# A new instruction order for a fused linear-attention and SoLU kernel: first loads and ScalarE's first logarithm moved

## Chip, cores and metric

The kernel runs on one core of a Trainium2 chip. The metric is the device time of one execution in microseconds (us), the median of several runs.

## The reference

Two layers. The first is a recurrent attention in the manner of RWKV-6 on B=4, H=8, S=768, D=48; the second a feed-forward layer with a SoLU activation and a layer norm on the 3072 tokens of 384 features that the first one gives.

```python
for t in range(S):
    kt, vt, rt, wt = (k[:, :, t], v[:, :, t], r[:, :, t], w[:, :, t])
    cur = np.einsum('bhd,bhe->bhde', u[None] * kt, vt)
    y[:, :, t] = np.einsum('bhd,bhde->bhe', rt, state + cur)
    state = wt[:, :, :, None] * state + np.einsum('bhd,bhe->bhde', kt, vt)
...
h = x @ w_in                                  # 384 -> 1024
e = np.exp(h - h_max)
sm = e / (np.sum(e, axis=-1, keepdims=True) + 1e-09)
solu = h * sm
ln = (solu - mu) / np.sqrt(var + 1e-06) * g_ln
return (ln @ w_out).astype(np.float32)        # 1024 -> 384
```

## The kernel before

The sequence is cut into six chunks of 128 tokens; a chunk of one batch is a unit, so there are 24 units (0 to 23). Units 0 to 3 are the first chunk of the four batches and have no state from before. Within a unit the recurrence is written as matrix products: prefix sums of the logarithm of w give decays, which scale k and r; masked products of r and k give a 128x128 score matrix for each head; a state of one 48x48 matrix for each head goes from chunk to chunk.

Every step of a unit is a small function (a stage), and a text that lists them one by one, `ORDER`, says in which order all stages are put into the program. A word of it is a stage's name, the unit's number, and after a dot what it uses: the engine (`a` ScalarE, `d` VectorE, `p` GpSimd) or the DMA queue (`s` SyncE, `a` ScalarE, `p` GpSimd), or the PSUM bank (`s0` to `s3` single banks, `b0` and `b1` double ones). Each engine is wrapped in `InOrder`, so that it takes its instructions in the order of the words; nothing reorders them. A stage that waits for data holds up all that stands behind it on its engine. [...]a stage that takes a slot waits until the one that had it before has been read.

The stages of a unit, with the engine that runs them:

- `LW`, `LK`, `LR`, `LV`: loads of w, k, r, v, 192 KB each, 192-byte rows.
- `lw` (ScalarE): the logarithm of w. `cum` (TensorE): prefix sums, two matmuls of 384 columns. `ex` (ScalarE): their exponential, in PSUM. `kp` (VectorE): k and r scaled by it.
- `p`, `q` (GpSimd), `dg` (VectorE), `dv` (GpSimd): the bonus term with u. `vb`: v rounded to bf16.
- `krk`, `krr` (TensorE): four transposes of the scaled k, four of the scaled r; `kr` copies them to SBUF. `KD` in place of these three: one DMA transpose, issued by SyncE.
- `M`: scores (eight matmuls); `m`: masked copy (VectorE in one step, or ScalarE and then `sel` on GpSimd).
- `Y`: attention output; `y` copies it, adding the bonus (`Y` with an `i` adds the bonus by a matmul, and then ScalarE may copy). `S`, `et`, `st`: the state.
- `X`, `xT`: transposition of the output and its copy; `XD`: the same by a DMA transpose.
- `H`: hidden matmuls (24 of 128 columns, or six of 512 for units that have an `HD`); `e`, `he`, `hq`: exponential, product, square; `HD`: DMA transpose of `he`. `Oa`, `Ob`: output matmuls in two halves; `sq`, `qm`, `lv`: the norm's scale; `o`: the scaled output; `out`: the store.

Once, in the opening: `pc` sets up constants (VectorE memsets and four masks on GpSimd), `hot` with a number runs so many matmuls of 512 columns on a constant tile, `LI`, `LO`, `wi`, `gw`, `mn` and `ce` bring in and prepare the two weight matrices, and `LU`, `ur`, `us`, `uc` spread u over all partitions.

The stage functions are defined inside one kernel function, and at its end a loop over `ORDER` calls them. The profile puts nearly all instructions on line 88, in the wrapper, so they are told apart by the tiles that they write and read: `lw<-w_in` is `lw`, `cum_ps<-cum_ps` is `ex`, `kp<-cum_ps,kr_in` is `kp`, `m<-m_ps,uts` is `m`, `kr_in<-in_k_dram` is `LK`. The stages that matter in the first microseconds are short:

```python
def log_w(i, x):
    act.activation(out=lw_t[i % NLW][:, :, :D], in_=w_t[i % NIO][:, :, :D], func=LN)
...
def load_w(i, x):
    queue[x].dma_start(out=w_t[i % NIO][:, :, :D], in_=rows_of(w, i))
...
for word in ORDER.split():
    word, _, how = word.partition(".")
    name = word.rstrip("0123456789")
    stages[name](int(word[len(name):]), how)
```

Of the kernel before, what the change touches and what calls it, by code (L numbers as in the profile page):

```python
# [26 lines left out]
dv1 m2.d wi1.p vb3.a xT0.d LR5.s dg3 wi2.a krk4.s0 vb2.p M3.b0 st1 krr4 q4 y1.d Y2.ns1 S2.s2 m3.d H0.b1 dv2
gw1.a LV4.p kr4.d et2 gw3.a LW6.s dg4 M4.b0 lw5 dv3 X1.s3 m4.d e0 hot3.s0 gw2.p gw0.a y2.d cum5.b0 LK6.s Y3.ns0
xT1.d gw4.a gw6.p S3.s1 y3.d X2.s3 gw5.a he0 LR6.s gw7.a ex5 mn0.s0 LW7.s st2 et3 xT2.a kp5 vb4.p hq0 H1.b1 dv4
ce4 LK7.s lw6 ce6 p5 ce1 cum6.b0 LR7.s X3.s2 ce7 krk5.s3 LV5.p ex6 ce3 krr5 LW8.s xT3.a kp6 q5 e1 S4.s2 LK8.s  # L30
ce5 H2.b0 LV6.p kr5.a he1 LR8.s lw7 krk6.s3 ce0 e2 H3.b1 LW9.s ce2 dg5 vb5.p hq1 LV7.p st3 krr6 Y4.is0 LK9.s he2
e3 Oa0.s1 p6 y4.a LR9.s kr6.d cum7.b0 lw8 Oa1.s0 vb6.p he3 et4 ex7 dv5 Ob0 LW10.s hq2 q6 kp7 X4.s3 hq3 LK10.s
M5.b1 p7 xT4.d M6.b0 m5.d krk7.s3 Ob1 sq0 m6.a q7 LR10.s qm0 dg6 krr7 lw9 cum8.b1 LV8.p kr7.d lv0 H4.b0 LW11.s
ex8 st4 p8 dg7 sq1 o0.a LK11.s Y5.ns3 qm1 kp8 e4 Oa2.s2 out0.p LR11.s y5.d q8 krk8.s1 lv1 cum9.b1 he4 krr8 LV9.s
ex9 Ob2 p9 kr8.d lw10 S5.s3 p10 hq4 kp9 Oa3.s1 LW12.s sel6 sq2 o1.d et5 lw11 M7.b0 LK12.s M8.b1 qm2 st5 m7.a Ob3
dv6 m8.d lv2 q9 cum10.b0 LR12.s sq3 X5.s0 Y6.ns3 o2.d ex10 vb7.p cum11.b1 xT5.d S6.s2 vb8.a out1 sel7 qm3 kp10
ex11 Oa4.s0 y6.d LW13.s LV10.p et6 lv3 H5.b0 st6 lw12 dg8 LK13.s o3.a dv7 kp11 X6.s3 krk9.s1 e5 LV11.p LR13.s
krk10.s2 krr9 xT6.d cum12.b1 dg9 LW14.s kr9.a Ob4 q10 he5 ex12 Y7.is3 LK14.s LV12.p dg10 krk11.s1 sq4 y7.a krr10
kp12 krr11 p11 kr10.a M9.b0 LR14.s S7.s3 m9.d dv8 H6.b1 hq5 p12 qm4 kr11.d et7 LW15.s lv4 S8.s2 st7 e6 vb9.p
X7.s1 o4.d LK15.s M10.b0 dv9 Y8.ns3 et8 xT7.d lw13 krk12.s0 he6 m10.a Oa5.s1 out2.p LR15.s vb10.p krr12 lw14  # L40
y8.d cum13.b0 p13 H7.b1 st8 LW16.s ex13 kr12.d q11 hq6 kp13 LK16.s S9.s3 LV13.p Y9.ns2 e7 dg11 LV15.s M11.b0
y9.d LV14.p X8.s0 Ob5 et9 m11.a he7 vb11.p krk13.s2 LR16.s lw15 M12.b0 q12 st9 xT8.a cum14.b1 m12.d sq5 krr13
LW17.s ex14 X9.s0 vb12.p Oa6.s3 sel10 xT9.a qm5 kp14 LK17.s cum15.b0 lv5 Ob6 dv10 ex15 kr13.d S10.s0 lw16 p14
kp15 hq7 M13.b1 LR17.s Y10.ns2 q13 H8.b0 sq6 et10 vb13.a qm6 o5.d LW18.s sel11 lv6 y10.d m13.a krk14.s1 st10
LK18.s Oa7.s2 q14 dg12 e8 o6.d krr14 LR18.s dv11 Y11.ns0 kr14.d lw17 cum16.b1 dv12 X10.s3 he8 Ob7 ex16 LW19.s
p15 S11.s1 LV16.s sq7 y11.d xT10.a H9.b0 hq8 out3.p kp16 LV17.s p16 et11 st11 X11.s0 H10.b1 e9 LK19.s dg13 p17
xT11.d lw18 qm7 he9 LR19.s q15 Y12.ns3 vb14.a krk15.s1 e10 S12.s0 vb15.p out4 y12.d krr15 dv13 lv7 M14.b0 kr15.d
Oa8.s3 m14.a sel13 he10 out5 X12.s1 lw19 M15.b0 LW20.s q16 et12 Ob8 m15.a st12 LK20.s dg14 p18 cum17.b1 dg15
H11.b0 out6 ex17 xT12.d sel14 o7.d hq9 kp17 out7 krk16.s0 Y13.ns1 vb16.p LR20.s sq8 e11 krr16 dv14 qm8 H12.b1
LW21.s kr16.d q17 hq10 y13.d LK21.s he11 krk17.s2 dv15 Oa9.s0 e12 LR21.s vb17.p Y14.ns1 lv8 he12 krr17 LW22.s  # L50
o8.a M16.b0 Ob9 lw20 kr17.d m16.a out8 cum18.b1 y14.d X13.s3 Oa10.s2 ex18 dg16 xT13.d dv16 sq9 hq11 S13.s1 kp18
X14.s3 sel15 M17.b0 xT14.d et13 hq12 KD18 Ob10 qm9 m17.d p19 cum19.b1 S14.s3 st13 ex19 q18 H13.b0 lv9 kp19 sel16
sq10 o9.a Y15.ns1 et14 e13 out9 st14 H14.b1 p20 LV18.s y15.d lw21 qm10 LV19.s he13 Oa11.s0 LK22.s e14 dg17
X15.s3 cum20.b0 lv10 xT15.d Y16.ns1 he14 Ob11 o10.a ex20 out10 vb18.p S15.s2 y16.d dv17 KD19 sq11 S16.s3 kp20
et15 hq13 cum21.b1 q19 S17.s1 qm11 st15 LV20.s H15.b0 et16 lv11 q20 st16 LR22.s ex21 dg18 vb19.a krk20.s2 kp21
Oa12.s3 et17 e15 st17 KD21 M18.b1 o11.a krr20 he15 X16.s1 Ob12 m18.a LW23.s kr20.d S18.s0 xT16.a HD14 sel18 sq12
lw22 M19.b0 qm12 M20.b1 m19.d Y17.ns2 m20.a vb20.p LK23.s Oa13.s1 dv18 LR23.s lv12 dg19 cum22.b0 y17.d H16.b1
dv19 LV21.s ex22 o12.d sel20 et18 kp22 X17.s2 HD15 S19.s3 e16 st18 p21 Ob13 xT17.d et19 he16 krk22.s0 p22 sq13
lw23 M21.b0 krr22 m21.a Y18.ns2 st19 q21 HD16 cum23.b1 qm13 kr22.d Y19.ns3 ex23 sel21 H17.b0 y18.d LV22.s lv13
y19.d o13.a kp23 X18.s0 Oa14.s2 e17 xT18.d KD23 M22.b1 dg20 Ob14 hq14 he17 dv20 X19.s3 Y20.ns1 vb21.p hq15  # L60
Oa15.s0 dg21 HD17 q22 y20.d H18.b0 xT19.d sq14 hq16 dv21 m22.d XD20 Ob15 p23 e18 dg22 Y21.ns1 out11 qm14 H19.b1
y21.d LV23.s vb22.a he18 lv14 XD21 dv22 Y22.ns3 e19 Oa16.s1 q23 y22.d out12 M23.b0 sq15 hq17 HD18 he19 Ob16
Oa17.s3 vb23.p hq18 dg23 out13 H20.b1 o14.d dv23 HD19 qm15 m23.d lv15 X22.s2 sq16 Ob17 e20 out14 xT22.d H21.b0
qm16 hq19 he20 Y23.ns2 sq17 e21 qm17 H22.b1 HD20 o15.d y23.d lv16 he21 lv17 Oa18.s0 e22 X23.s2 Ob18 HD21 xT23.d
hq20 Oa19.s2 he22 Ha23.b0 sq18 hq21 Ob19 qm18 o16.d HD22 o17.d Hb23 lv18 Oa20.s1 sq19 out15 ea23 o18.d out16
hq22 Oa21.s3 hea23 out17 Ob20 qm19 out18 eb23 Ob21 lv19 heb23 Oa22.s0 sq20 hqa23 qm20 o19.d sq21 lv20 Ob22 qm21
# [559 lines left out]
```

## Time and profile before

| | us |
|---|---|
| median of 13 runs | 146.43 |
| lowest, highest | 145.34, 147.23 |
| the profiled execution, its own time | 146.29 |
| its span, first to last instruction | 144.2 |
| TensorE matmul busy (PE) | 130.3 |
| VectorE busy (DVE) | 126.2 |
| ScalarE busy (ACT) | 123.8 |
| GpSimd busy (POOL) | 102.0 |

The span is what the profiler sees; some 2.1 us of the execution's own time lie around it. Busy time counts each engine's own instructions. Matmuls are pipelined and their ends are modelled, so PE's busy time is more than the time for which the array needs the work. Idle time of an engine that isn't the limit in a stretch costs nothing there. In the lines below, what stands behind `<-` in brackets is what ended the idle time before an instruction, and `ACTq` or `SPq` marks the issue of a DMA by that engine's queue.

### The profile page before, as it was taken

To read this page: it belongs to the slowest core of one execution; us is meant where nothing else is said; L and a number is where in the kernel's file an instruction comes from. 1 tells how busy PE (TensorE), PEld (TensorE's weight loads), DVE (VectorE), ACT (ScalarE), POOL (GpSimd) and SP (SyncE) were. 2 spreads that over 40 slices of the span, in tenths; PEclk is the share of its full clock that TensorE was granted. 3 is DMA by queue.
4 is the path that set the end of the run, shared out by engine and by line. 5 is a ranking of instruction groups with operands and counts; after the bars stand their busy time and mean duration, and the time that the engine had idled before them with its cause. 6 is when DMAs were issued, how large, how long until landed. Compare 5 with 4: busy or idle time off the path is not lost.

```text
span 144.2 us, 4709 instructions
## 1 busy us (share of the span) xinstructions
PE 130.3 (90%) x1824; PEld 95.4 (66%) x1832; DVE 126.2 (88%) x239; ACT 123.8 (86%) x269; POOL 102.0 (71%) x128
## 2 busy tenths in 40 slices
...
PEclk9999965999999999999999999999999999999999
DMA  4999999999989989998999997859999998979934
GB/s 92 270 260 265 307 400 364 249 183 258 257 169 212 225 187 219 273 218 183 219 182 238 251 239 154 184 123 208 148 213 145 215 125 193 226 173 107 268 135 164
DMA packets 105623, 30.65 MB, mean 213 GB/s; under 512 B 100553, under 2 KB 104402, under 8 KB 105602
## 3 DMA queue, kind: packets, MB, share of 16 engines
...
q10 hardware_dynamic: 4322, 0.89, 2.9%
...
## 4 chain that ended last, share of the span: by engine, by line
PE 73%; DVE 9%; DMA 6%; issue 5%; POOL 3%; ACT 1%; SPq 1%; DVEq 0%; POOLq 0%
PE o_ps L88 23%; PE h_ps L88 21%; PE y_ps L88 6%; PE kr_ps L88 5%; PE s_ps L88 5%; PE m_ps L88 5%; PE cum_ps L88 4%; DMA hq<-he 3%; DVE kp L88 3%; DMA kr_in<-in_k_dram 3%; PE x_ps L88 2%; DVE m L88 2%; DVE w L88 1%; POOL p L88 1%; DVE dg L88 1%
## 5 line engine op out<-in xcount | busy, mean ns | idle before, releaser
L88 DVE TENSOR_TENSOR he<-h_ps,e 128x1024 bf16<-128x1024 f32 (+1 forms) x25 | 29.4, 1175 | 1.8 <-ACT e L88 1.2
L88 PE MATMUL o_ps<-w,he 128*128 128x385 bf16 (+2 forms) x136 | 29.2, 306 | 0.5 <-DVE qm L88 0.5
L88 DVE TENSOR_TENSOR kp<-cum_ps,kr_in 128x768 bf16<-128x768 f32 x24 | 22.8, 950 | 5.1 <-ACT cum_ps L88 3.2
L88 ACT ACTIVATE e<-h_ps 128x1024 bf16<-128x1024 f32 (+1 forms) x25 | 24.7, 988 | 2.5 <-PE h_ps L88 2.3
L88 POOL TENSOR_TENSOR p<-kr_in 128x384 bf16<-128x384 f32 x24 | 23.8, 1001 | 4.2 <-DMA kr_in<-in_k_dram 2.8
L88 PEld LDWEIGHTS <-hq 128*128 128x128 bf16 x192 | 17.9, 97 | 12.6 <-DMA hq<-he 1.2
L88 PE MATMUL h_ps<-xT,win_sb 128*128 128x128 bf16 x360 | 23.7, 224 | 0.6 <-DVE kp L88 0.6
L88 POOL TENSOR_TENSOR dv<-vb,dg 128x384 bf16<-128x384 bf16 x24 | 19.8, 827 | 5.9 <-DVE dg L88 4.8
L88 PEld LDWEIGHTS <-win_sb 128*128 128x128 bf16 x360 | 22.0, 101 | 1.5 <-issue 0.7
L88 ACT ACTIVATE cum_ps<-cum_ps 128x768 f32<-128x768 f32 x24 | 19.2, 799 | 4.3 <-PE cum_ps L88 2.6
L88 POOL TENSOR_TENSOR q<-p,u_bc 128x384 bf16<-128x384 bf16 x24 | 21.8, 912 | 0.1
L88 PE MATMUL o_ps<-inv_col,e 128*128 128x1 bf16 x120 | 19.3, 165 | 0.0
L88 PE MATMUL o_ps<-one_col,hq 128*128 128x1 bf16 x120 | 19.1, 163 | 0.0
L88 PEld LDWEIGHTS <-kp 128*128 128x128 bf16 x240 | 15.4, 99 | 4.7 <-DVE xT L88 1.3
L88 DVE TENSOR_TENSOR m<-m_ps,uts 128x1024 bf16<-128x1024 f32 x13 | 15.8, 1216 | 1.9 <-PE m_ps L88 1.9
L88 PE MATMUL kr_ps<-ident,kp 128*128 128x128 bf16 x160 | 15.4, 228 | 1.6 <-DVE xT L88 1.0
L88 ACT ACTIVATE hq<-he 128x1024 bf16<-128x1024 bf16 (+1 forms) x16 | 15.9, 1003 | 0.0
L88 ACT ACTIVATE lw<-w_in 128x384 bf16<-128x384 f32 x24 | 12.6, 527 | 3.1 <-DMA w_in<-in_w_dram 3.1
L88 PE MATMUL o_ps<-w,hq 128*128 128x385 bf16 x72 | 13.9, 328 | 0.8 <-DMA hq<-he 0.8
L88 POOL TENSOR_SCALAR_AFFINE_SELECT m<-m 128x1024 bf16<-128x1024 bf16 x11 | 11.9, 1086 | 3.5 <-ACT m L88 3.5
L88 PEld LDWEIGHTS <-kr 64*128 64x128 bf16 (+1 forms) x272 | 10.7, 96 | 5.4 <-issue 1.4
L88 DVE TENSOR_REDUCE dg<-q 128x8 f32<-128x384 bf16 x24 | 12.9, 542 | 0.9 <-POOL q L88 0.9
...
## 6 DMA issues: line engine op xcount, KB each, us to landing
...
```

What stands on the lines that cost most here:

```text
L88: made = make(*args, **kwargs)
```

## The change

Only the text `ORDER` differs: 912 words become 904, in a new order. The stage functions, tiles and buffers are the same. The first lines of the two texts:

```diff
-pc0 LU0.a LR0.s LW1.a LW0.s hot7.s3 LK0.s LK1.s LV0.p ur0 LW3.s LR2.s lw0 LW2.a cum0.b0 lw1 hot1.s3 LR1.a LW4.s
-cum1.b1 p0 ex0 us0.s0 hot2.s3 LV1.p LK2.a kp0 ex1 vb0.p krk0.s1 LK3.s uc0 hot3.s3 lw2 LR3.s LG0.a cum2.b0 p1 kp1
-krr0 hot3.s3 kr0.a LK4.s q0 LR4.s ex2 M0.b1 LV2.p krk1.s2 dg0 S0.s3 lw3 m0.d krr1 et0 hot5.s1 vb1.a LV3.p lw4
+LV0.p LV1.p pc0 LR0.s LW0.a LU0.a LK0.s hot6.s3 LW2.s LK1.s lw0 LW1.a cum0.b0 LR1.a hot2.s3 ex0 ur0 LW3.s us0.s0
+hot3.s3 p0 kp0 uc0 lw1 LK3.s LK2.a cum1.b1 LR2.a krk0.s1 lw2 vb0.a cum2.b0 ex1 p1 LW4.s krr0 LR3.s LG0.a S0.s2
+kp1 vb1.p LK4.s hot3.s3 ex2 q0 kr0.a LR4.s LV2.p dg0 et0 lw3 M0.b1 kp2 p2 S1.s3 krk1.s0 LI0.s lw4 m0.d cum3.b0
...
```

By engine, the first instructions are now:

- GpSimd issues the loads of v for units 0 and 1 ahead of its four masks. Before, the masks came first, then v of unit 0, `p0`, and v of unit 1.
- ScalarE issues w of unit 0 and u, then runs `lw0`, then issues w and r of unit 1, and runs `ex0`, `uc0`, `lw1`. Then it issues k and r of unit 2 and runs `lw2`, `vb0`, `ex1`, `ex2`, `kr0`. Before, it issued u and w of unit 1, ran `lw0`, issued w of unit 2, ran `lw1`, issued r of unit 1, ran `ex0`, issued k of unit 2, and ran `ex1`, `uc0`, `lw2`, `kr0`, `ex2`.
- SyncE issues r and k of unit 0, w of unit 2, k of unit 1, w and k of unit 3. Before: r, w and k of unit 0, k of unit 1, w of unit 3, r of unit 2.
- VectorE runs `kp0 kp1 dg0 kp2 m0 dg1 kp3 st0 kp4 m1 m2`. Before: `kp0 kp1 dg0 m0 kr1 kp2 st0 m1 dg1 y0 kp3`.

Counted over the whole text, these kinds of words change:

| stage | before | after |
|---|---|---|
| matmuls in `hot` | 24 | 17 |
| `krk` and `krr` (TensorE), and `kr` (ScalarE, VectorE) | 20, 20, and 6, 14 | 18, 18, and 5, 13 |
| `KD` (DMA transposes): units | 18, 19, 21, 23 | 18 to 23 |
| `X`; `XD`: units | 22; 20, 21 | 21; 20, 21, 22 |
| `xT` on ScalarE, VectorE | 6, 16 | 14, 7 |
| `m` on ScalarE (with `sel`), VectorE | 11, 13 | 10, 14 |
| `y` on ScalarE, VectorE | 2, 22 | 3, 21 |
| `o` on ScalarE, VectorE (whole rows) | 8, 15 | 10, 13 |
| `vb` on ScalarE, GpSimd | 7, 17 | 4, 20 |
| `gw` on ScalarE, GpSimd | 6, 2 | 5, 3 |
| `LV` on GpSimd, SyncE | 14, 10 | 15, 9 |
| `out` on GpSimd, SyncE | 3, 20 | 4, 19 |

The order of the rest changes throughout, by a few places here and there.

More of the change, by code (lines that the diff above doesn't have):

```diff
@@ L21 @@
 ORDER = """
-pc0 LU0.a LR0.s LW1.a LW0.s hot7.s3 LK0.s LK1.s LV0.p ur0 LW3.s LR2.s lw0 LW2.a cum0.b0 lw1 hot1.s3 LR1.a LW4.s
-cum1.b1 p0 ex0 us0.s0 hot2.s3 LV1.p LK2.a kp0 ex1 vb0.p krk0.s1 LK3.s uc0 hot3.s3 lw2 LR3.s LG0.a cum2.b0 p1 kp1
-krr0 hot3.s3 kr0.a LK4.s q0 LR4.s ex2 M0.b1 LV2.p krk1.s2 dg0 S0.s3 lw3 m0.d krr1 et0 hot5.s1 vb1.a LV3.p lw4
-kr1.d LI0.s p2 kp2 LI1.s gs0.s0 cum3.b1 q1 LI2.s S1.s1 st0 ex3 LO0.s M1.b0 Y0.ns2 q2 m1.d LW5.s krk2.s3 gc0 krr2
-LO1.s dv0 kr2.a LK5.s dg1 cum4.b0 p3 y0.d ex4 kp3 X0.s0 p4 et1 wi0.a dg2 M2.b1 krk3.s2 kp4 q3 Y1.ns3 krr3 kr3.a
@@ L27 @@
[L27 to L66, printed above, removed]
@@ L67 @@
-out19 hqb23 o20.d Sa23.s2 sq22 lv21 qm22 out20 Mal23.s1 lv22 Sb23 o21.d sq23 o22.a Mar23.s3 out21 qm23 Mbl23
-lv23 out22 Mbr23 ol23.a or23.d outl23.a outr23
+LV0.p LV1.p pc0 LR0.s LW0.a LU0.a LK0.s hot6.s3 LW2.s LK1.s lw0 LW1.a cum0.b0 LR1.a hot2.s3 ex0 ur0 LW3.s us0.s0
+hot3.s3 p0 kp0 uc0 lw1 LK3.s LK2.a cum1.b1 LR2.a krk0.s1 lw2 vb0.a cum2.b0 ex1 p1 LW4.s krr0 LR3.s LG0.a S0.s2
+kp1 vb1.p LK4.s hot3.s3 ex2 q0 kr0.a LR4.s LV2.p dg0 et0 lw3 M0.b1 kp2 p2 S1.s3 krk1.s0 LI0.s lw4 m0.d cum3.b0
+q1 krk2.s1 LI1.s ex3 krr1 krr2 LW5.s p3 dg1 cum4.b1 kr1.a LI2.s kp3 LO0.s LV3.p ex4 gs0.s0 st0 LO1.s M1.b0 vb2.a
@@ new lines @@
+LK5.s dv0 kp4 krk3.s2 gc0 et1 kr2.a q2 m1.d krk4.s0 wi0.a M2.b1 p4 Y0.is1 m2.d krr3 y0.a q3 kr3.a X0.s1 krr4 dv1
+kr4.d LR5.s xT0.a M3.b0 lw5 dg2 S2.s2 LV4.p M4.b1 m3.d Y1.ns0 LW6.s hot3.s1 wi2.a wi1.p m4.d et2 q4 H0.b0 dg3
+gw2.p gw0.a y1.d dg4 e0 X1.s1 cum5.b1 xT1.d Y2.ns0 dv2 ex5 he0 vb3.p gw1.a gw3.p S3.s1 LK6.s gw6.a st1 H1.b0
+gw7.a y2.d LR6.s gw5.p st2 et3 gw4.a st3 X2.s3 e1 LW7.s kp5 dv3 mn0.s0 vb4.a he1 LV5.p xT2.a LK7.s lw6 S4.s2 hq0
+dv4 ce4 krk5.s1 Y3.is3 LR7.s ce0 cum6.b1 p5 y3.a ce6 krr5 ex6 X3.s3 ce7 LW8.s H2.b0 LV6.p ce1 et4 xT3.a kp6
@@ new lines @@
+kr5.a LK8.s p6 Y4.is3 ce2 e2 H3.b1 vb5.p ce3 LR8.s LV7.p ce5 hq1 he2 krk6.s1 LW9.s Oa0.s0 q5 e3 st4 krr6 LV8.p
+LK9.s y4.a M5.b0 he3 lw7 Ob0 lw8 vb6.p hq2 kr6.d X4.s2 q6 LR9.s cum7.b1 S5.s3 m5.d sq0 LV9.p ex7 Oa1.s1 LW10.s
+xT4.a qm0 kp7 p7 M6.b0 lv0 Ob1 m6.a dg5 LK10.s krk7.s2 o0.d cum8.b1 dv5 hq3 krr7 dg6 H4.b0 kr7.d LR10.s sq1 dv6
+et5 ex8 qm1 st5 vb7.p lw9 Y5.ns0 LW11.s kp8 vb8.p e4 Oa2.s2 LV10.p y5.d cum9.b1 lv1 he4 krk8.s3 LK11.s ex9 sel6
+Ob2 o1.a LR11.s kp9 krr8 q7 lw10 M7.b0 X5.s1 sq2 m7.a Oa3.s0 kr8.d LW12.s vb9.p dg7 p8 M8.b1 qm2 LK12.s xT5.d
@@ new lines @@
+lw11 cum10.b0 m8.d krk9.s3 dv7 lv2 Ob3 ex10 p9 o2.d LR12.s S6.s1 hq4 kp10 cum11.b1 q8 krr9 LW13.s Y6.ns2 sq3
+ex11 qm3 kr9.d H5.b0 out0.p et6 lv3 y6.d LK13.s vb10.p kp11 o3.a q9 X6.s3 Oa4.s2 lw12 LR13.s st6 e5 out1.p dg8
+cum12.b1 LW14.s Ob4 p10 xT6.d ex12 he5 krk10.s1 LK14.s sq4 S7.s0 q10 lw13 qm4 krr10 kp12 hq5 S8.s3 sel7 M9.b0
+LR14.s dg9 et7 H6.b1 et8 lv4 kr10.d out2.p m9.a LW15.s st7 dv8 st8 Y7.ns1 o4.a krk11.s0 sel9 y7.d krk12.s3 e6
+krr11 LK15.s dg10 M10.b0 X7.s1 kr11.d dv9 m10.a Y8.ns2 krr12 LR15.s he6 S9.s0 p11 xT7.a cum13.b0 lw14 LW16.s
@@ new lines @@
+S10.s1 et9 y8.d ex13 q11 H7.b1 kr12.d et10 hq6 p12 st9 LK16.s kp13 X8.s2 Y9.ns3 LV11.p xT8.a Oa5.s0 LR16.s e7
+st10 y9.d p13 cum14.b0 LW17.s Ob5 he7 ex14 p14 X9.s1 lw15 LK17.s Oa6.s2 kp14 sq5 hq7 LV12.p LR17.s M11.b1 qm5
+M12.b0 m11.a sel10 Ob6 m12.d lv5 krk13.s3 LW18.s dv10 cum15.b1 sq6 dg11 xT9.a krr13 H8.b0 ex15 qm6 vb11.p kr13.d
+LK18.s q12 lw16 kp15 Y10.ns1 LR18.s LV13.p e8 krk14.s3 o5.d H9.b1 dg12 lv6 LV14.p y10.d LW19.s o6.a he8 krr14
+vb12.p e9 S11.s0 LV15.s sel11 X10.s1 krk15.s2 xT10.d lw17 M13.b0 kr14.d Oa7.s1 m13.a LK19.s q13 he9 krr15 et11
```

22 lines of the change are left out of this document (added).

## The prediction

> **What bounds the kernel now.** I read the busy shares first, then the chain of waits, then three stretches cut where the chain changes character, and last the opening engine by engine.
>
> ```profile
> PE 130.3 (90%) x1824; PEld 95.4 (66%) x1832; DVE 126.2 (88%) x239; ACT 123.8 (86%) x269; POOL 102.0 (71%) x128
> PEclk9999965999999999999999999999999999999999
> DMA  4999999999989989998999997859999998979934
> ...
> PE 73%; DVE 9%; DMA 6%; issue 5%; POOL 3%; ACT 1%; SPq 1%; DVEq 0%; POOLq 0%
> ```
>
> ```profile
> 0.00:38.40 38.40, 29.45 (x341) 20.12 (x344) 29.94 (x74) 26.88 (x44) 30.40 (x43) 0.91 1.07 265
> 38.40:126.40 88.00, 87.69 (x1362) 66.62 (x1364) 85.28 (x144) 83.39 (x182) 71.56 (x86) 1.00 0.98 198
> 126.40:144.20 17.80, 13.21 (x129) 8.70 (x128) 10.96 (x22) 13.54 (x47) 0.00 (x0) 1.00 0.75 170
> ```
>
> Averages say "three engines nearly full". The stretches say more (after the length: PE, weight loads, DVE, ACT, POOL, clock, DMA share, GB/s). From the first output matmuls of unit 0 (Oa0, 38.4 us) to the hidden matmuls of unit 22 (H22, 126.4 us) PE is busy 87.69 of 88.00 us, so there the time is PE's work. ACT (83.39) and DVE (85.28) have only 3 to 5 us of room. Before 38.4 us PE is not the limit; after 126.4 us the last units drain. So the change is three sums: when Oa0 starts, how much PE work follows, and whether the drain differs.
>
> The opening, as the timeline shows it (start, length, engine):
>
> ```profile
> 5.19 0.52 ACT L88 ACTIVATE lw<-w_in 128x384 bf16<-128x384 f32 x1 [3.12 <-DMA w_in<-in_w_dram]
> 5.67 0.52 ACT L88 ACTIVATE lw<-w_in 128x384 bf16<-128x384 f32 x1
> 6.33 1.66 ACTq L88 DMA_DIRECT2D kr_in<-in_k_dram  x1
> 8.03 0.80 ACT L88 ACTIVATE cum_ps<-cum_ps 128x768 f32<-128x768 f32 x1 [0.93 <-PE warm_ps L88]
> ...
> 9.89 0.96 DVE L88 TENSOR_TENSOR kp<-cum_ps,kr_in 128x768 bf16<-128x768 f32 x1 [1.80 <-DMA kr_in<-in_r_dram]
> 12.26 1.22 DVE L88 TENSOR_TENSOR m<-m_ps,uts 128x1024 bf16<-128x1024 f32 x1
> 13.99 0.95 DVE L88 TENSOR_TENSOR kp<-cum_ps,kr_in 128x768 bf16<-128x768 f32 x1
> ...
> 26.39 1.22 DVE L88 TENSOR_TENSOR m<-m_ps,uts 128x1024 bf16<-128x1024 f32 x1 [1.61 <-PE m_ps L88]
> ```
>
> The two logarithms (lw0, lw1) run back to back. The exponential of unit 1 (8.03) is put down to PE, but the matmuls it needs ended near 6.8 us; what stood before it on ACT was the issue of one load, 1.66 us until 7.99. From 12.26 us DVE works almost without a pause, and the chain runs mostly over DVE until 34.7 us.
>
> **What the Trainium skill says.** *DMA: Bandwidth & Descriptors*, "Issuing engines are not separate DMA queues": loads from SyncE, ScalarE and GpSimd interleave on the same 16 engines, so a second queue saves only issue time, "usually small relative to the DMA itself". The trace agrees on the sharing (253 to 273 GB/s from 4 to 16 us, whichever queue issues: a 192 KB load, 0.197 MB, each 0.75 us). It differs on issue time: 1.66 us here. *TensorE: Matmul & The Clock Gate*, the table at its head: ScalarE, VectorE and GpSimd take instructions strictly in order; the late exponential behind the load is that. The same page, "Back-to-back issue gap": a 128-column matmul costs N/2.4 + 2.5 ns, 56 ns; here 24 hidden matmuls take 1.34 us in the chain, 56 ns each. Its Part 1: the clock halves after a window of about 3.4 us with little PE work; here the granted clock was 0.50 from 20 to 24 us.
>
> **The change, part by part.** The program's code is the same but for the order text, so counts of words give the work and their places give the waits.
>
> 1. *v loads first on GpSimd.* Two issues of 1.08 and 0.92 us move from 2.28 and 7.12 us to the start; the four masks slide behind them, from 1.4 to about 2.6 us. The first user, the prefix sum of unit 0, runs at 5.3 us: hidden. But v0 and v1 now go ahead of w2, k1 and the rest in the shared engines: later loads slip by up to two transfers, 1.5 us. Within POOL, 1.08 us leave the stretch before p1.
>
> 2. *lw0 ahead of the loads.* ACT now issues w0 and u_row, then lw0, then w1 and r1. w0 goes out at 0.8 instead of 1.31 us, so lw0 starts near 4.9, not 5.19: 0.3 us won for unit 0. But w1, issued at 1.38 before, now stands behind lw0's wait: issue 4.9, plus the 3.8 us median of the w loads to landing, is 8.7. So lw1 starts at 8.7, against 5.67: 3.0 us late.
>
> 3. *k2 and r2 both on ACT, behind lw1.* Before, r2 was SP's (issued 5.14) and k2 ACT's (6.33). Now both are issued after lw1, ahead of lw2, the copy of v0, and the exponential ex1. An issue from ACT took 0.57 us (r1) to 1.66 (k2); two end at 9.9 to 12.1, I take 11.0. Then lw2 0.52 and vb0 0.51: ex1 12.0 to 12.8, against 8.03 to 8.83. So kp1 runs at 12.8 instead of 9.89, dg0 until 14.2. r2, issued near 9.7 and landing 4.1 (r1) to 6.5 us (k2) later, is there at 13.8 to 16.2; I take 14.8.
>
> 4. *New order on DVE.* kp2 now stands before the mask multiplication m0, and the prefix sum cum3 takes the slot b0 that kp2 must have left: kp2 14.8 to 15.7, m0 15.7 to 16.9 (before: 12.26 to 13.48), cum3 15.8 at the earliest (before: 13.91). Before, kp0, kp1, dg0, m0, kr1 and kp2 were done at 14.94. Now the same without kr1 (0.68, moved to ACT) is done at 16.9: DVE is 2.0 us late. ACT is late as well: ex2 until 13.6 and kr0 until 14.6, where both were done by 12.15; of the 2.5 us, 0.5 is vb0, which ACT has done in addition.
>
> 5. *What the opening gives back.* Ahead of Oa0 the new list has less DVE work: y0 (0.55) and xT0 (0.35) go to ACT, and the 1.61 us wait before m4 was slack. ACT has 0.8 us more ahead of Oa0, by the same count (kr1, y0, xT0 and others come, gains and copies go). ACT stood idle some 5.6 us between 12 and 38 us, in eight pieces; about half can absorb lateness, the rest waits for loads that come no earlier. About 2.0 late on either, plus 0.7 for ACT's longer list, less 1.5: Oa0 starts 1.2 us late. Ends: 0, if idle pieces take all of it; +3.0, if nothing does.
>
> 6. *Seven warm-up matmuls fewer* (24 to 17): at 0.43 us each cold and 0.216 warm they fill PE idle time; nothing while the clock holds, see the second rival.
>
> 7. *Units 20 and 22 turned by DMA.* PE loses 16 transposes of 56 ns, 0.89 us, and three for x of unit 22, 0.17; one more bonus matmul of 384 columns adds 0.16. Net -0.9 us in the stretch where PE is full. DVE loses one kr copy of 0.68 and one xT of 0.35, ACT one kr of 1.01. SP gets three transpose issues of about 1.26 us, landing 2.7 to 3.3 us after issue. Between turned kr20 and its user M20 stand about 4 us of PE work: just enough. For unit 22 there is more. If kr20 comes late, PE loses up to 1 us.
>
> 8. *Copies moved.* By kinds: eight xT more on ACT (+3.9), one y (+0.5), two o (+1.15), three vb fewer (-1.5), one m (-1.0), one kr (-1.0), one gain (-0.6): ACT +1.4 in all; between Oa0 and H22 the words give +1.4 too (0.8 more before, 0.9 less after). So ACT there goes from 83.39 to about 84.8 us in a stretch that shrinks to 87.1. DVE falls by 4.3 in all (nine xT, two o, one y, one kr fewer, one m more). POOL +3.2 stays under all others. ACT still fits, with half the room; I charge 0.4 us of new stalls on PE (ends: -0.3, since DVE is freer, and +1.5).
>
> 9. *The drain.* From H22 to the end the same units' words follow in nearly the same order; o of the last half moves from DVE (0.42) to ACT (0.42). Nothing, within 0.5 us either way.
>
> Sum against the profiled execution (span 144.2, its own time 146.29, 0.14 under the median): +1.2 - 0.9 + 0.4 + 0 = +0.7, so 147.0 us.
>
> **The rivals.** *Opening hidden (not slower).* ACT's second load issue is quick and r2 lands by 13.8; the idle pieces take the lateness; PE's 0.9 us less stays. For it: PE idles some 15 us before 38.4, and what is late at 15 us needn't be at 38. Against it: PE needs kp and kr in order, and DVE had few gaps. It decides from the point where Oa0 starts by 38.7: opening +0.2, middle -0.9, 145.6 us. *The clock and ACT (slower still).* With fewer warm-up matmuls and unit 1 late by 3 us, PE has under 1 us of work from 7.5 to 11 us; the clock may fall before 15 us and stay down while some 6 us of PE work lies between M0 and H0. At half clock that is 6 us more, perhaps a quarter unhidden: +1.5 on the forecast, 148.5. Against it: the trace before shows the clock back after 6 us. *That the order isn't what runs* is excluded: each engine takes its instructions in the order written.
>
> **Numbers.** Forecast 0.45 (its own range 146.2 to 147.9), opening hidden 0.40, clock and ACT 0.15. About 0.3% (0.44 us) is what a measurement of this kernel can tell from no change. Of the forecast's case and of the hidden one I give 0.15 each to that band: slower 0.53, same 0.13, faster 0.34. The range reaches from the hidden case with the favourable middle (145.6 - 0.8) to the clock case with some of the ACT bound (148.5 + 0.7): 144.8 to 149.2.
>
> **What would show it.** lw1 near 8.7, ex1 near 12, m0 near 15.7, Oa0 near 39.6 confirm the opening. If Oa0 starts at or before 38.4, it is wrong. PE's stretch from Oa0 to H22 should be about 87.5 us; 87.1 or less means the transposes are saved whole, over 88.5 means ACT or kr20 stalls PE. A PEclk digit under 8 before 15 us speaks for the clock.

## The result: slower, and all of it in the opening

| | before | after |
|---|---|---|
| median of the runs taken together (48 and 11), us | 146.59 | 148.71 |
| ratio, with its 95% interval | | 1.0133 [1.0105, 1.0162] |
| the profiled execution, its own time, us | 146.29 | 148.76 |
| its span, us | 144.2 | 146.7 |

The forecast was 147.0, its own range 146.2 to 147.9, and the range over all cases 144.8 to 149.2. The measured median lies above the forecast's own range and inside the wide one. The ratios here and below leave out executions more than 1.5% slower than the fastest of their kernel, which the medians count, so the two can differ by up to 0.9%; the profiles of three kernels below (loads as before; k2, r2 and gains on SyncE with v back; more warm-up matmuls) are of such slow executions.

From the page of the kernel after, the lines that answer to those shown of before:

```profile
PE 130.2 (89%) x1800; PEld 93.8 (64%) x1807; DVE 123.0 (84%) x227; ACT 124.1 (85%) x274; POOL 104.8 (71%) x133
...
PEclk9995995599999999999999999999999999999997
DMA  4999999999799999999979997969599999688853
...
PE 59%; ACT 11%; DMA 9%; SPq 6%; POOL 5%; issue 4%; DVE 2%; DVEq 0%; ACTq 0%; POOLq 0%
```

The three stretches again, cut where Oa0 and H22 start. The prediction's cut at 126.4 us, which it calls H22, lies inside the hidden matmuls of unit 21 (126.01 us); H22 starts at 127.81 before and at 130.43 after. Before and after with these cuts (length, then PE, weight loads, DVE, ACT, POOL with their counts, clock, DMA share, GB/s; the opening of before is the prediction's first line):

```profile
38.40:127.80 89.40, 89.05 (x1378) 67.46 (x1380) 86.56 (x147) 84.79 (x186) 71.56 (x86) 1.00 0.98 199
127.80:144.20 16.40, 11.85 (x115) 7.86 (x112) 9.69 (x21) 12.14 (x41) 0.00 (x0) 1.00 0.72 164
```

```profile
0.00:41.10 41.10, 30.29 (x334) 19.66 (x336) 28.25 (x69) 27.48 (x47) 30.33 (x41) 0.88 1.03 253
41.10:130.40 89.30, 88.08 (x1356) 66.35 (x1360) 85.47 (x138) 85.03 (x191) 74.50 (x93) 1.00 0.96 200
130.40:146.70 16.30, 11.87 (x121) 7.83 (x116) 9.30 (x21) 11.54 (x38) 0.00 (x0) 0.94 0.67 184
```

The opening takes 41.1 us instead of 38.4, the middle 89.3 instead of 89.4, the drain 16.3 instead of 16.4: +2.7, -0.1, -0.1, together the 2.5 us by which the span grew. In the middle PE is busy 0.97 us less and idle 0.87 us more (89.40 - 89.05 = 0.35 before, 89.30 - 88.08 = 1.22 after), so the two nearly cancel.

ScalarE in the first microseconds of the kernel after, from the timeline:

```profile
8.78 0.52 ACT L87 ACTIVATE lw<-w_in 128x384 bf16<-128x384 f32 x1 [1.26 <-DMA w_in<-in_w_dram]
10.32 0.39 ACTq L87 DMA_DIRECT2D kr_in<-in_k_dram  x1
11.08 0.38 ACTq L87 DMA_DIRECT2D kr_in<-in_r_dram  x1
11.50 0.52 ACT L87 ACTIVATE lw<-w_in 128x384 bf16<-128x384 f32 x1 [2.20 <-DMA kr_in<-in_k_dram]
...
12.33 0.79 ACT L87 ACTIVATE cum_ps<-cum_ps 128x768 f32<-128x768 f32 x1
14.57 0.30 ACTq L87 DMA_DIRECT2D g_rows<-in_moe_g_ln_dram  x1
14.98 0.80 ACT L87 ACTIVATE cum_ps<-cum_ps 128x768 f32<-128x768 f32 x1 [1.85 <-DVE dg L87]
15.68 1.02 ACT L87 COPY kr<-kr_ps 128x1024 bf16<-128x1024 bf16 x1
```

And VectorE:

```profile
13.16 0.96 DVE L87 TENSOR_TENSOR kp<-cum_ps,kr_in 128x768 bf16<-128x768 f32 x1 [5.62 <-ACT cum_ps L87]
14.03 0.54 DVE L87 TENSOR_REDUCE dg<-q 128x8 f32<-128x384 bf16 x1
15.80 0.96 DVE L87 TENSOR_TENSOR kp<-cum_ps,kr_in 128x768 bf16<-128x768 f32 x1 [1.23 <-ACT cum_ps L87]
17.20 1.23 DVE L87 TENSOR_TENSOR m<-m_ps,uts 128x1024 bf16<-128x1024 f32 x1 [0.44 <-PE m_ps L87]
```

The telling lines are the two issues at 10.32 and 11.08 and the logarithm lw2 at 11.50. The issues are short (0.39 and 0.38 us), but ScalarE stood idle for about a microsecond ahead of the first (lw1 ends at 9.30) and for 0.37 us between the two, and lw2, which reads only w, is put down to a load of k. So the wait belongs to the issues that stand ahead of lw2. The same happens at 14.57, ahead of ex2: the load of the gains, 4 KB, is issued 1.45 us after ex1 is done (13.12). The label at ex2 names DVE's dg, but dg ran from 14.03 to 14.57 and ex2 reads nothing of it; the chain of waits of the kernel after says what the issue waited for:

```profile
10.21 4.33 DMA kr_in<-in_k_dram
14.55 0.02 issue
14.57 0.30 ACTq L87
...
14.98 0.80 ACT cum_ps L87
15.78 0.02 issue
15.80 0.97 DVE kp L87
16.77 0.38 PE m_ps L87 x8
```

A load of k for unit 4, issued by SyncE at 10.21, holds ScalarE's issue of an unrelated small load until it has landed, and with it ex2, the copy kr0, the scores and m0. (kp2 is in the chain too, but r of unit 2, which it reads as well, lands only at 15.27.)

The built program explains the pairs. In it the loads issued by SyncE and ScalarE take one of eight completion semaphores in turn, and a load waits, before it is issued, until the earlier load on its semaphore has landed (GpSimd's loads have semaphores of their own). Which two share one depends on the order in which the built program lists these loads. That isn't the order of the words, and it comes out different when loads are moved, those of GpSimd too. The earlier load of each of ScalarE's late ones, from the built programs:

```
load on ScalarE   before   after   v back in after   v first in before
k of unit 2       k0       w3      k1                w2
r of unit 2       (SyncE)  k3      w3                (SyncE)
gains             w3       k4      w4                r1
```

The landings in the trace of after fit the pairs: w3 lands at 10.30 and k2's issue starts at 10.32; k3 lands at 11.05 and r2's issue starts at 11.08; k4 lands at 14.54 and the gains' issue starts at 14.57. Before, ScalarE's issues of k2 (6.33) and of the gains (8.82) follow at once on what stands ahead of them, without such a wait. The issue of k2 itself took 1.66 us there, although k0 had landed at 6.03; so an issue can also be long for a reason other than this wait, and that reason stays open. The Trainium skill, *DMA: Bandwidth & Descriptors*, "Anatomy of one DMA — SWDGE (gpsimd) path", says that the DMA engines don't wait on semaphores and that any such wait happens on the issuing sequencer before dispatch; here the sequencer is ScalarE's, and the exponentials queue behind it (ex1 at 12.33, ex2 at 14.98).

### The profile page after: what moved, and what is told of

It reads as the page before. It is cut to its first block, busy times and chain, and to the rows that moved or that the text cites. A ratio compares the mean times of both kernels' runs of the same rounds, so it can differ in the third digit from the quotient of the medians.

```text
span 146.7 us, 4656 instructions
## 1 busy us (share of the span) xinstructions
PE 130.2 (89%) x1800; PEld 93.8 (64%) x1807; DVE 123.0 (84%) x227; ACT 124.1 (85%) x274; POOL 104.8 (71%) x133
## 4 chain that ended last, share of the span: by engine, by line
PE 59%; ACT 11%; DMA 9%; SPq 6%; POOL 5%; issue 4%; DVE 2%; DVEq 0%; ACTq 0%; POOLq 0%
PE o_ps L87 17%; PE h_ps L87 16%; SPq L87 6%; PE m_ps L87 5%; PE s_ps L87 5%; ACT e L87 5%; PE kr_ps L87 4%; PE y_ps L87 4%; PE cum_ps L87 4%; DMA hq<-he 3%; DMA kr_in<-in_k_dram 3%; DMA out_dram<-o 3%; PE x_ps L87 2%; POOL dv L87 2%; ACT cum_ps L87 1%
## 5 line engine op out<-in xcount | busy, mean ns | idle before, releaser
L87 PE MATMUL h_ps<-xT,win_sb 128*128 128x128 bf16 x360 | 23.0, 220 | 1.4 <-DVE he L87 1.3
L87 PEld LDWEIGHTS <-win_sb 128*128 128x128 bf16 x360 | 21.1, 99 | 2.6 <-issue 2.1
L87 DVE TENSOR_TENSOR m<-m_ps,uts 128x1024 bf16<-128x1024 f32 x14 | 17.0, 1218 | 1.9 <-PE m_ps L87 1.8
L87 POOL TENSOR_SCALAR_AFFINE_SELECT m<-m 128x1024 bf16<-128x1024 bf16 x10 | 10.9, 1094 | 6.1 <-ACT m L87 6.1
L87 PE MATMUL kr_ps<-ident,kp 128*128 128x128 bf16 x144 | 13.9, 226 | 0.8 <-DVE kp L87 0.8
L87 PEld LDWEIGHTS <-he 128*128 128x128 bf16 x136 | 12.6, 96 | 1.3 <-DVE o L87 0.2
```

The source lines that it names most:

```text
L87: made = make(*args, **kwargs)
```

## The theories and the experiments

Five theories stood against each other. WAIT: ScalarE's load issues wait for earlier loads to land and hold its computations. TRANSFER: v put first pushes all later data back in the shared engines, whoever issues it. LOADS: the opening's loads as a whole, not the order of computations. ORDER: the new order of computations costs the opening its time. CLOCK: fewer warm-up matmuls, and PE at half speed. All kernels below compute the whole reference; they differ from one of the two kernels in words of `ORDER` alone. Times of the starts (lw1, ex1, kp2, m0, H0, Oa0) are from one profiled execution of each.

| kernel | median us (runs) | ratio to before [95%] | ex1 | kp2 | m0 | H0 | Oa0 |
|---|---|---|---|---|---|---|---|
| before | 146.59 (48) | | 8.03 | 13.99 | 12.26 | 23.51 | 38.42 |
| after | 148.71 (11) | 1.0133 [1.0105, 1.0162] | 12.33 | 15.80 | 17.20 | 28.20 | 41.08 |
| loads as before | 147.41 (20) | 1.0001 [0.9969, 1.0032] | 10.92 | 13.96 | 14.82 | 25.52 | 38.30 |
| v back | 145.31 (4) | 0.9877 [0.981, 0.9943] | 10.15 | 13.62 | 14.49 | 24.27 | 37.16 |
| w1 ahead of lw0 | 148.44 (7) | 1.0084 [1.0035, 1.0134] | 12.48 | 15.93 | 17.53 | 28.25 | 41.00 |
| gains later | 147.25 (20) | 1.0058 [1.0033, 1.0084] | 12.31 | 15.56 | 16.44 | 26.76 | 39.52 |
| k2, r2 elsewhere | 147.17 (20) | 1.0016 [0.9985, 1.0046] | 10.75 | 13.91 | 15.30 | 25.52 | 38.28 |
| k2, r2, gains on SyncE | 147.22 (20) | 0.997 [0.9937, 1.0003] | 10.46 | 13.22 | 14.23 | 24.13 | 39.08 |
| the same, v back | 147.05 (22) | 1.0005 [0.9974, 1.0036] | 9.61 | 13.12 | 13.99 | 23.43 | 37.69 |
| before with v first | 148.77 (5) | 1.0158 [1.0113, 1.0202] | 10.04 | 15.70 | 13.96 | 25.19 | 40.10 |

### The opening's loads against the order of computations

The loads of the opening get the queues of before and nearly its places; the computations stay in the new order. The one exception is v of unit 1, which stands ahead of p0 on GpSimd and is issued at 3.37 us, where before has 7.12.

```diff
-LV0.p LV1.p pc0 LR0.s LW0.a LU0.a LK0.s hot6.s3 LW2.s LK1.s lw0 LW1.a cum0.b0 LR1.a hot2.s3 ex0 ur0 LW3.s us0.s0
-hot3.s3 p0 kp0 uc0 lw1 LK3.s LK2.a cum1.b1 LR2.a krk0.s1 lw2 vb0.a cum2.b0 ex1 p1 LW4.s krr0 LR3.s LG0.a S0.s2
+pc0 LU0.a LR0.s LW1.a LW0.s hot6.s3 LK0.s LK1.s LV0.p LW3.s LR2.s lw0 LW2.a cum0.b0 LR1.a LW4.s hot2.s3 ex0 LV1.p
+LK2.a ur0 us0.s0 hot3.s3 p0 kp0 LK3.s uc0 lw1 cum1.b1 krk0.s1 lw2 vb0.a cum2.b0 ex1 p1 krr0 LG0.a LR3.s S0.s2 kp1
```

> The changed kernel with the opening's loads back in the queues and places of the kernel before (r, w, k of unit 0 and w of unit 1 first, v0 and v1 behind the masks and p0, r2 on SyncE, k2 on ScalarE behind ex0); the order of the compute is the new one. Theory LOADS (ScalarE's own loads, waiting for earlier loads to land, hold up its exponentials): lw1 back near 6 to 7 us, kp2 near 14, Oa0 at 39.0 or earlier, 146.0 to 147.0 us. Theory ORDER (kp2 ahead of m0, and H0 behind M4, Y1 and three warm-up matmuls, cost the opening whatever the loads do): Oa0 stays at 40.5 or later, 148.2 to 148.9. Theory CLOCK (PE halves its clock for want of early work): in between, 147.2 to 148.2, with a PEclk of 5 still in the opening.

The first output matmul of before, of after and of this kernel:

```profile
38.42 0.33 PE L88 MATMUL o_ps<-w,he 128*128 128x385 bf16 x1
41.08 0.33 PE L87 MATMUL o_ps<-w,he 128*128 128x385 bf16 x1
38.30 0.33 PE L86 MATMUL o_ps<-w,he 128*128 128x385 bf16 x1
```

Oa0 is back where it was, and the ratio is 1.0001. ORDER falls as the cause of the late opening. By the medians of all runs 0.8 of the 2.1 us remain (147.41 against 146.59), so the loads are most of the loss, and that they are all of it isn't shown. The early stages did not come as expected: lw1 starts at 9.50, not at 6 to 7 us, because the issue of k2 (6.94, 2.15 us long, k0 having landed at 6.29) and the copy of u stand ahead of it. H0 is 2.0 us later than before, and Oa0 isn't.

### v of units 0 and 1 back in their places

```diff
-LV0.p LV1.p pc0 LR0.s LW0.a LU0.a LK0.s hot6.s3 LW2.s LK1.s lw0 LW1.a
+pc0 LR0.s LW0.a LU0.a LK0.s hot6.s3 LW2.s LK1.s LV0.p lw0 LW1.a
...
-hot3.s3 p0 kp0 uc0 lw1
+hot3.s3 p0 LV1.p kp0 uc0 lw1
```

> The changed kernel with only v0 and v1 back behind the masks and p0 on GpSimd. LOADS, if the two early v transfers push the others back: w1 and r1 land 0.7 to 1.5 us earlier, 147.8 to 148.3 us. If the v loads were harmless: 148.4 to 149.0.

At 145.31 us in four runs this is the fastest kernel of all, faster than both, and faster than either theory had it. Its ScalarE, from the timeline:

```profile
8.25 0.52 ACT L86 ACTIVATE lw<-w_in 128x384 bf16<-128x384 f32 x1 [0.75 <-DMA w_in<-in_w_dram]
8.26 0.37 ACTq L86 DMA_DIRECT2D kr_in<-in_k_dram  x1
8.76 0.51 ACTq L86 DMA_DIRECT2D kr_in<-in_r_dram  x1
9.31 0.52 ACT L86 ACTIVATE lw<-w_in 128x384 bf16<-128x384 f32 x1 [0.54 <-DMA w_in<-in_w_dram]
...
10.15 0.79 ACT L86 ACTIVATE cum_ps<-cum_ps 128x768 f32<-128x768 f32 x1
11.75 0.31 ACTq L86 DMA_DIRECT2D g_rows<-in_moe_g_ln_dram  x1
12.16 0.80 ACT L86 ACTIVATE cum_ps<-cum_ps 128x768 f32<-128x768 f32 x1 [1.22 <-DVE kp L86]
```

The logarithm lw1, which waits for data, comes 0.53 us earlier than after (8.25 against 8.78). The issue of k2 comes 2.06 us earlier (8.26 against 10.32) and that of the gains 2.82 us (11.75 against 14.57). Two things lengthen ScalarE's waits when v goes first. Other loads land later: w2 at 7.31 instead of 5.93, k1 at 8.46 instead of 7.33, w3 at 10.30 instead of 8.74, slips of 1.1 to 1.6 us. And the pairs are others: k2 waits for w3 instead of k1, r2 for k3 instead of w3, the gains for k4 instead of w4, each time a load that lands later. No run here separates the two. From Oa0 to the end it takes as long as after (105.7 and 105.6 us); only the opening differs, by 3.9 us.

### v first, in the kernel before

```diff
-pc0 LU0.a LR0.s LW1.a LW0.s hot7.s3 LK0.s LK1.s LV0.p ur0
+LV0.p LV1.p pc0 LU0.a LR0.s LW1.a LW0.s hot7.s3 LK0.s LK1.s ur0
...
-ex0 us0.s0 hot2.s3 LV1.p LK2.a kp0
+ex0 us0.s0 hot2.s3 LK2.a kp0
```

> The kernel before with only v0 and v1 issued first on GpSimd. There ScalarE issues k2 and g behind lw1; with v first they share a semaphore with w2 and r1 instead of k0 and w3. WAIT: k2's issue holds ScalarE until w2 lands, near 9, so ex1 slips from 8.0 to 9 or later, and the time is 1 to 2.5 us longer, 147.6 to 149.1. TRANSFER: 1 to 1.5 us longer at kp1 and less at the end, 146.7 to 147.6.

It costs 1.6% here, alone. On ScalarE's timeline of this kernel the two logarithms run together, late by about a microsecond, and k2's issue, which follows ex0, waits:

```profile
6.61 0.52 ACT L87 ACTIVATE lw<-w_in 128x384 bf16<-128x384 f32 x1
...
9.62 0.37 ACTq L87 DMA_DIRECT2D kr_in<-in_k_dram  x1
10.04 0.80 ACT L87 ACTIVATE cum_ps<-cum_ps 128x768 f32<-128x768 f32 x1 [1.66 <-PE warm_ps L87]
```

lw1 is 0.94 us later than before (6.61 against 5.67) and k2's issue 3.29 (9.62 against 6.33). The earlier load on its semaphore was w2, issued only at 6.19 and landed at 9.60. Of the delay of k2's issue 1.3 us is the later ex0 ahead of it (7.59 against 6.30), which is late data, and the rest is the wait; the time is in WAIT's range. Here too the label at the exponential names PE, while it was the issue that came last.

### No load of k2, r2 and the gains on ScalarE, with v first and with v back

The second kernel has this edit and that of v back.

```diff
-LK2.a cum1.b1 LR2.a
+LK2.s cum1.b1 LR2.s
...
-LR3.s LG0.a S0.s2
+LR3.s LG0.s S0.s2
```

> The changed kernel, v0 and v1 still first, with k2, r2 and the gains g issued by SyncE at the same places of the order, so that ScalarE issues nothing behind lw0 but w1 and r1 and waits for no earlier load. Theory WAIT (each of these three issues waits on ScalarE until an earlier load that shares its completion semaphore has landed: w3, k3, k4): lw2 near 9.3, ex1 near 10.3, m0 near 15 to 16, 146.0 to 147.4 us. Theory TRANSFER (v0 and v1 merely push all later loads back in the 16 engines): kp2 stays near 15.5 because r2 lands as late, 148.0 to 148.9.

> As the run before, and with v0 and v1 back behind the masks and p0 on GpSimd: the difference between the two is the v loads alone, with no wait on ScalarE between. WAIT: under 1 us apart. TRANSFER: 1.5 to 3 us apart. In either case the fastest or near it: 144.5 to 146.0 us.

With ScalarE free of these waits, v may stay first: ex1 follows two logarithms and a copy at 10.46, and the ratio is 0.997 instead of 1.0133. (By the medians of all runs 0.6 us of the loss remain, 147.22 against 146.59.) Put back or not, v now makes 0.2 us in the medians (147.22 and 147.05), against 3.4 us with the issues on ScalarE (148.71 and 145.31). In the profiles there remains something of TRANSFER (lw1 0.69 us, Oa0 1.4 us later with v first), but no difference in the times that the intervals can tell from none. So later data alone costs no time that shows; it costs through ScalarE's waits for it, and WAIT carries most of the loss. The second kernel's time lies above the 144.5 to 146.0 us that either theory gave it.

These two kernels are not as fast as the one with v back alone, and the chain of waits of the first shows what is late next:

```profile
17.43 9.98 DMA wout_f<-in_moe_w_out_dram
```

SyncE, with three more loads to issue, gets to the output weights (two loads of 768 KB) at 17.43, where after it was 16.06, and the first of them lands at 27.41, where after it was 24.72. From there the chain runs through the scaling of these weights to Oa0. Once unit 0's way to m0 is short, H0 at 24.1 is no longer what sets Oa0 at 39.1. With v back alone this landing ends the wait as well (28.35 us), and still Oa0 starts at 37.16, so it isn't the only thing. That part stays open.

### k2 and r2 in places of before

r2 goes back to SyncE, behind w3, and k2, still on ScalarE, to behind ex0.

```diff
-ex0 ur0 LW3.s us0.s0
+ex0 LK2.a ur0 LW3.s LR2.s us0.s0
...
-LK2.a cum1.b1 LR2.a krk0.s1
+cum1.b1 krk0.s1
```

> The changed kernel with r of unit 2 back on SyncE (behind w3) and k of unit 2 back on ScalarE behind ex0; v0 and v1 stay first, lw0 stays ahead of the load of w1. LOADS, k2 and r2 being the larger part: ex1 near 10.5, kp2 near 14, 147.0 to 147.7 us. If the late lw1 alone sets the opening: 148.2 to 148.9. ORDER or CLOCK: 148.3 or more.

1.2% come back (1.0133 to 1.0016), and Oa0 at 38.28 is that of the kernel before, although v is still first and ex1, at 10.75, is 2.7 us later than before. The wait has moved: k2 now shares its semaphore with w1, which lands at 8.70, and its issue starts at 8.72. It holds the copy of u and lw1 (9.51), but lw1 reads w1 and couldn't have run before 8.70 anyway.

### The gains later

```diff
-LR3.s LG0.a S0.s2
+LR3.s S0.s2
...
-kr0.a LR4.s
+kr0.a LG0.a LR4.s
```

> The changed kernel with the 4 KB load of the gains (g) moved behind the copy kr0 on ScalarE, so that ex2 and kr0 don't wait for it. LOADS: ex2 at 13.1 instead of 14.98, kr0 done by 15, kp2 then held by r2 at 15.3: 0.4 to 1.0 us won, 147.7 to 148.3 us. ORDER or CLOCK: kp2 and what follows are late anyway, 148.5 to 148.9.

ex1 is where it was (12.31), and ex2 follows it at once (13.04 instead of 14.98). kp2 hardly moves, because now r of unit 2 holds it:

```profile
15.56 0.96 DVE L86 TENSOR_TENSOR kp<-cum_ps,kr_in 128x768 bf16<-128x768 f32 x1 [1.00 <-DMA kr_in<-in_r_dram]
```

But kr0 is done 2 us earlier, m0 comes 0.8 us and Oa0 1.6 us earlier, and the ratio falls by 0.75%. One issue of 4 KB in the wrong place cost about a microsecond. In this edit the pairs of k2 and r2 stay as they were, so it is the cleanest test of a single wait.

### w1 ahead of the first logarithm

```diff
-LW0.a LU0.a
+LW0.a LW1.a LU0.a
...
-lw0 LW1.a cum0.b0
+lw0 cum0.b0
```

> The changed kernel with the load of w of unit 1 ahead of the first logarithm, as before. If the late lw1 is the cause: lw1 near 6, kp1 near 10, and 147.0 to 147.8 us. If the loads k2 and r2 ahead of lw2 are (LOADS by another wait): lw1 is early, yet ex1 stays near 12, and the time falls by 0.5 at most: 148.2 to 148.8.

lw1 starts at 8.48 instead of 8.78, so the edit did not make it early, and ex1 and Oa0 hardly move; the ratio is 1.0084, with an interval that overlaps that of after. lw1 stands behind the copy of u, which ran at 8.10 here; and ex1 waits for the two issues behind lw1 (k2 at 9.76, r2 at 11.23), r2's until k3 lands at 11.21. Since that landing would hold ex1 even behind an early lw1, the place of w1 should cost next to nothing in this order; that is argued from this trace and not shown by a run with an early lw1.

This kernel also speaks on CLOCK. PE's stretches, after first and then this kernel (columns as above):

```profile
12.00:15.00 3.00, 2.92 (x18) 1.43 (x17) 1.42 (x2) 1.15 (x4) 1.24 (x2) 0.50 1.26 256
...
22.00:25.00 3.00, 2.75 (x31) 1.85 (x32) 1.93 (x3) 2.49 (x5) 3.00 (x4) 0.50 1.06 366
25.00:28.50 3.50, 3.28 (x38) 2.14 (x40) 3.50 (x5) 2.24 (x5) 3.50 (x5) 0.50 1.00 240
```

```profile
12.00:15.00 3.00, 2.77 (x18) 1.43 (x17) 1.42 (x2) 1.28 (x3) 1.05 (x2) 1.00 1.25 255
...
22.00:25.00 3.00, 2.00 (x26) 1.30 (x27) 2.98 (x3) 2.72 (x7) 3.00 (x4) 0.77 1.06 371
25.00:28.50 3.50, 3.41 (x47) 2.35 (x49) 2.58 (x4) 3.17 (x6) 3.50 (x5) 0.71 0.90 218
```

After was profiled at half clock (0.50, the column behind POOL's count) in all three, this kernel at 1.00, 0.77 and 0.71. Yet H0 starts at 28.20 in after and 28.25 here, and Oa0 at 41.08 and 41.00: the half clock of that execution didn't decide when its opening ended.

### Warm-up matmuls: more, and fewer

First six more behind krk0, and nine for three behind k4's load; then the three ahead of H0 taken out.

```diff
-hot3.s3 ex2 q0 kr0.a
+hot9.s3 ex2 q0 kr0.a
...
-krk0.s1 lw2
+krk0.s1 hot6.s3 lw2
```

```diff
-LW6.s hot3.s1 wi2.a
+LW6.s wi2.a
```

> The changed kernel with twelve more warm-up matmuls, in PE's two idle stretches (six at about 10 us, three made nine at about 13.5 us). CLOCK: PEclk stays at 9 up to 16 us and is less long at 5 between 22 and 28, H0 starts 1 us or more earlier, 147.3 to 148.2 us. LOADS or ORDER: the early clock rises and the time doesn't move, 148.4 to 149.0.

> The changed kernel without the three warm-up matmuls between Y1 and H0, which took 1.3 us of PE at half clock just ahead of H0. If PE is the limit there (CLOCK): H0 starts 0.8 to 1.3 us earlier, 147.5 to 148.2 us. If H0 waits for a copy of weights or another engine: 148.5 to 148.9, and H0 where it was, near 28.4.

More of them: 146.85 us (20 runs), ratio 1.0016 [0.9987, 1.0046], 1.2% better than after. Fewer: 149.16 us (4 runs), 1.0188 [1.0151, 1.0224], 0.5% worse, with intervals that overlap; H0 came 0.5 us earlier and Oa0 0.4 us later. Both times lie outside what any theory gave, and the first is nearest to CLOCK's. So more of them are worth something in this order. Each run also reports its mean clock, and for the kernel with more of them time follows it: 145.9 to 146.6 us in the nine runs at 0.994 or above, 147.5 to 149.6 in the six at 0.975 or below. Of the kernel after, two runs were at 0.996 or above, at 148.71 and 147.26 us; seven runs of the kernel before at 1.00 took 145.0 to 145.6. So even near full clock after is about 2 us slower or more, and CLOCK alone doesn't explain its loss; with two runs of after, a share of it isn't excluded. More warm-up matmuls win back nearly as much as moving the loads does, and in their profile ScalarE's waits are those of after (issues of k2, r2 and the gains at 10.25, 11.00 and 14.46, Oa0 at 41.20). Where their gain arises isn't shown.

### Units 20 and 22 turned on TensorE again, and by DMA in the kernel before

In after:

```diff
-st15 KD20
+st15 krk20.s0 krr20.s0
...
-et16 hq13
+et16 kr20.a hq13
...
-xT17.d KD22
+xT17.d krk22.s3 krr22.s3 kr22.d
...
-H20.b1 o14.d hq18 HD18 he19 Oa16.s2 vb23.a qm15 et19 XD22 e20
+H20.b1 X22.s2 o14.d xT22.d hq18 HD18 he19 Oa16.s2 vb23.a qm15 et19 e20
```

In before the reverse: `KD20`, `KD22`, `XD22` in place of `krk`, `krr`, `kr`, `X` and `xT` of these units.

> The changed kernel with units 20 and 22 turned on PE again (16 transposes and kr copies, and x of unit 22), in place of the DMA transposes. If the transposes by DMA saved PE's 0.9 us: 149.2 to 149.7, the stretch from Oa0 to H22 0.6 to 1.0 us longer. If kr20 by DMA comes late and stalls PE as much as it saves: 148.4 to 148.9.

> The kernel before with k and r of units 20 and 22 and the output of unit 22 turned by DMA, all else as it was. If the DMA transposes save what PE no longer does: 145.2 to 145.9 us. If they save more than PE's 1.06 us, as putting PE's transposes into the changed order cost 2.2: 143.8 to 145.0. If they stall M20 or H22: 146.5 or more.

In after it costs 1.6% (150.91 us of 4 runs, 1.0291 [1.0245, 1.0338]): from Oa0 to H21 it takes 90.1 us instead of 87.7, PE busy 88.36 instead of 86.53. That is more than the two theories gave, and more than the 1.06 us of the transposes; the rest isn't explained. In before the opposite edit costs 1.7% as well (149.18 us of 4 runs, 1.0173 [1.0131, 1.0215]), as the last of the three expectations, a stall, had it. What PE waited for there between 95 and 130 us (total, times, longest):

```profile
PE m_ps L86 <- DMA kr<-kp: 1.6, 2, 0.8
```

And the same of the kernel after:

```profile
PE m_ps L87 <- DMA kr<-kp: 0.6, 1, 0.6
PE o_ps L87 <- DMA hq<-he: 0.3, 1, 0.3
```

For before the same view lists no wait. In this kernel the turned k and r of a unit come 3.2 to 3.9 us after the issue; in the order of before not enough PE work lies between the issue and the scores, and two waits of 0.8 us eat what PE saves. From Oa0 to H21 it takes 89.1 us here and 87.6 before; another 0.7 us is lost after H21 (18.9 against 18.2), and where isn't shown. The DMA transposes pay in one order and cost in the other, so their price alone can't be told from these two.

## Why the prediction was right in sign, and what its sum missed

| step | as predicted | measured |
|---|---|---|
| 1. later loads slip | up to 1.5 us | 0.5 us (w1) to 1.6 us (w3), after against v back |
| 2. lw0, lw1 | 4.9, 8.7 | 4.35, 8.78 |
| 3. ex1, kp1 | 12.0 to 12.8, 12.8 | 12.33, 13.16 |
| 4. kp2, m0 | 14.8, 15.7 | 15.80, 17.20 |
| 4. ex2 until, kr0 until | 13.6, 14.6 | 15.78, 16.70 |
| 5. opening | +1.2 (0 to +3.0) | +2.7 |
| 7. PE work from Oa0 to H22 | -0.9 | -0.97 |
| 8. new stalls of PE there | +0.4 (-0.3 to +1.5) | +0.87 |
| 9. drain | 0 | -0.1 |

**The steps that held.** Up to ex1 and kp1 the times came as forecast, and step 7's PE work and the drain did. Step 8's stalls were twice the forecast, 0.87 us, of which 0.6 is a late turned k and r, which step 7 had named; so the middle won 0.1 us and not 0.5. The forecast's sign came from late k2 and r2 on ScalarE, and the experiment that moves these two takes 1.2 of the 1.33% away. lw1's 8.78 against 8.7 is in part luck: w1 went out 0.55 us earlier than forecast (4.35) and took 4.4 us to land instead of 3.8.

**The term that was mis-sized** is the opening, +1.2 us in the sum, +2.7 measured, inside the ends of step 5. The missing 1.5 us are already there at m0 (17.20 against 15.7 forecast). Two things made it. Step 3 priced a load on ScalarE as issue time, 0.57 to 1.66 us from the rows of before, and two of them as ready at 11.0; the issues took 0.39 and 0.38 us and were waits, until 10.32 and 11.08, for other loads. The end, 11.46, was close to the 11.0 by luck. And step 4 charged nothing for the third, the load of the gains ahead of ex2, which the list of ScalarE's instructions under the change leaves out too: it waited 1.45 us and made ex2 and kr0 about 2 us late. Without it m0 comes at 16.44, 0.8 us earlier, and the time falls by 0.75%. The rest of m0's delay is kp2, which with or without that wait stays near 15.7, since r2, issued at 11.08 after its own wait, lands at 15.3 to 15.5 where step 3 took 14.8.

**Step 1** looked at v's data and found that later loads slip by up to 1.5 us, which came true (w3 by 1.6), but it gave this no price in the sum. What it did not look for is where the slip is paid: ScalarE's issues wait for loads that land later, and two loads moved on a third queue also change which loads share a semaphore on the other two. Together this makes 3.4 us of median in after, and 1.6% in before. Step 2's cost, lw1 3 us late, came true in time and, as far as the traces tell, was worth next to nothing, since ex1 had other waits.

**Step 5** expected idle pieces to take half of the lateness. With m0 4.9 us later than before (17.20 against 12.26, and 3.4 forecast), H0 is 4.7 us late (28.20 against 23.51); only after H0 nearly half of it is taken back, and Oa0 is 2.7 late.

**Step 6** said nothing for the warm-up matmuls. The order turned out to depend on them: 1.2% for more, and perhaps 0.5% for fewer. The rival of the clock, whose sign in the profile (a clock digit under 8 before 15 us) did appear and whose 148.5 is the nearest figure to the measured one, isn't the whole cause: near full clock after stays behind by about 2 us or more, and an execution with a higher clock in the opening ended it as late (41.00). A share of it stays open. The rival of the hidden opening, 145.6, falls with Oa0 at 41.08.
